# Weight sums stored in pieces of 512 bytes, their last twelve pieces in a slot of their own, and one query-weight tile in layer 1

## The chip, the core and the metric

The kernel runs on one core of one Trainium2 chip. The metric is the device time of one execution in microseconds (us), lower is better. Three runs of the kernel before took 2207.41, 2213.9 and 2215.41 us; the median is 2213.9.

Engine names in the profile: PE is the matrix engine (PEld its weight loads), DVE the vector engine, ACT the scalar engine, POOL the general engine that here only clears small regions and issues transfers, SP the queue that only issues transfers. Each engine, and each issuing queue, works through its instructions in the order in which they were written.

## The reference

Two layers, each of attention and then a feed-forward network, on 2048 tokens of width 576. The same weights serve both layers.

```
x = x + attention(layernorm(x))      # 32 heads of 18; each token looks at 8 earlier ones, 2 apart
x = x + silu(layernorm(x) @ w1) @ w2 # 576 -> 4608 -> 576
(the same two lines again)
```

Everything is in float32; the kernel gets there with pairs of fp16 halves (a high and a low part of every operand).

## The kernel before

**Stages.** The 2048 tokens are cut into four chunks of 512, so there are eight stages: stages 0 to 3 are the chunks of layer 0, stages 4 to 7 those of layer 1. A stage is attention, projection (`project`, L859 on PE, L866 on DVE), layer norm, transposition, and the feed-forward network (`ffn`). The attention of stage s+1 is meant to run on DVE while PE does the feed-forward products of stage s, and its projection lies on PE between the products of stage s.

**Two ways to the first product.** In stages 0 to 2 a tile of 128 hidden units is one run of 14 matmuls of 512 columns (L1118). From stage 3 on (`SF = 3`) two such tiles are done together by seven products in place of eight (`pair_z`, L1045: seven matmuls of 256 columns each). That needs sums and differences of the four quarters of the weights of a pair: seven combinations, each in a high and a low fp16 part. They are made once and kept in device memory, in `wts[p]` for the pairs p = 0 to 17, and loaded again by `load_wt` in every stage from 3 on (SP, L1020). The second product is L1131, and DVE adds its result to the residual at L866.

**Making the weight sums.** `prepare(p, k, t, prio, after)` does one third of a pair (k = 0, 1: 128 rows; k = 2: the last 32 rows, four times). There are 54 such pieces. Each takes a buffer ("slot") and runs

- a load of raw weights, issued by POOL (L984, L987),
- four additions on DVE (L993 to L996), the scaled high part on ACT (L998), the low part on DVE (L1003); the last one is kept in the list `preps`,
- a store into `wts[p]`, issued by POOL (L1009 for the high part, L1011 for the low part, which k = 2 has not).

The slots that a piece can have: `pw`, three of them, in the arenas `ra` and `rb`; `pk`, the two key and value tiles `kv`; `po`, the tiles `o` and `pr` of attention. Pieces 0 to 23 (`EARLY = 24`) use `pw` alone, later ones go round `pw`, `pk` and `po`. The names in the trace are those of the memory: `ra`, `rb`, `kv`, `o`, `pr`.

**Layer 1's attention.** `load_wq` (L635) loads the query, key and value weights of one of four units (8 heads each) into a `wq` tile; there are two, one in `ra` and one at the end of `rb`. The second lies in memory that every second transposed activation tile (`xt`) also uses. The load and the clearing of the `kv` tile's edge (L741, L742) are made to wait for `preps[-4:]`, the last four of the 54 pieces, because `kv`, `o` and `pr` are theirs until then. L690 is the matmul of the unit, L756 and L758 move its result to `kv` and `qt`, L768 copies the rows of neighbours, and L787 to L828 is the attention on DVE.

**What sets the order.** A planner (`Plan`) takes all operations with a guessed duration, a priority and, for transfers, a number of bytes (`nbytes`), plays them through, and writes the instructions in the order that results: each free engine takes the ready operation of the best priority whose buffers are free. So a changed cost or a changed slot moves instructions on every engine from the first piece of weight sums on.

```
def prepare(p, k, t, prio, after):
...
        op("POOL", 1.2 if k < 2 else 2.4, load, [], [(r, 0)], prio, nbytes=P * 4 * P * 6, after=after)
...
            nc.gpsimd.dma_start(d[:, :, k, :], cut_(0))
```

`wts[p]` is laid out so that the seven combinations are outermost and the five thirds (three high, two low) inside, each 128 numbers: a store writes 256 bytes at a time.

Of the kernel before, what the change touches and what calls it, by code (L numbers as in the profile page):

```python
# [16 lines left out]
P = 128  # L17
# [19 lines left out]
HT = TB // 2  # L37
HD = D // 2
SF = 3
PREP = 1.2  # L40
STEP = 1
LATE = 0.2
EARLY = 24
LNS = 512.0
HSH = 2.0 ** -5

# [229 lines left out]
def sliding_attention_silu_ffn(ctx: ExitStack, tc: tile.TileContext, x, wqkv, wo, w1, w2, out):  # L276
    nc = tc.nc
# [5 lines left out]
    op = S.op  # L283
# [8 lines left out]
    def T(b):  # L292
        return S.tags[b.tag][b.slot]
# [10 lines left out]
    def cut(a):  # L304
        return lambda v: v.rearrange("p (a b) -> p a b", a=a)
# [3 lines left out]
    QW, XW = 30 * UC, 9 * TB  # L309
    shared("ra", QW, [])  # L310
    shared("rb", 3 * XW + QW, [
        ("wq", [("ra", 0, QW), (3 * XW, 3 * XW + QW)], cut(10), True),
        ("xa", [(XW * i, XW * (i + 1)) for i in range(3)], cut(9), True),
        ("xl", [(0, XW), (35 * HT, 35 * HT + XW)], cut(9), True),
        ("x0", [(XW, 2 * XW)], cut(9), True),
# [315 lines left out]
        op("POOL", 2.8 if w.kind == "h" else 0.6, store, w.keys, [("wqs", u)], -0.6, nbytes=P * 20 * QR, after=marks[m:m + 1])  # L631

    def load_wq(u, prio):
        w = Unit("wq")
        op("SP", 0.4, lambda: nc.sync.dma_start(fl(T(w.bufs[0])), wqs[u]), [("wqs", u)], w.keys, prio, nbytes=P * 20 * QR,  # L635
           after=turned[-2:] + preps[-4:])
        return w

    WQ = (-9, -8, -7, -6)
# [81 lines left out]
    def attention(s, xT, wq, more=None):  # L721
# [4 lines left out]
        for u in range(NU):  # L726
            kv, qt = Buf("kv"), Buf("qt")
            own = [(kv, j) for j in range(NJ)]
            if wq is None:
                def fetch(kv=kv, qt=qt, u=u):  # L730
                    row = blk * TB
                    nc.scalar.dma_start(T(kv).rearrange("p a b c -> p (a b c)"),
                                        rows(kd[par][u], row, [[NJ * 2 * UC, P], [1, NI * 2 * UC]]))
                    nc.scalar.dma_start(fl(T(qt)), rows(qd[par][u], row, [[NJ * UC, P], [1, NJ * UC]]))
                op("ACT", 1.4, fetch, [("qd", c, u), ("qd0", u) if blk == 0 else ("eds", lay, par, u)],
                   own + [(qt, j) for j in range(NJ)] + [(kv, "halo"), (kv, "edge")], pr_, nbytes=P * 4 * UC * 26)
            else:
                w = wq(u)
                if blk == 0:
                    def clear(kv=kv):  # L740
                        nc.gpsimd.memset(T(kv)[0:2, 0:3], 0.0)  # L741
                        nc.gpsimd.memset(T(kv)[0:1, 3:7], 0.0)  # L742
                    op("POOL", 1.6, clear, [], [(kv, "edge")], pr_, after=turned[-2:] + preps[-4:])
                else:
                    def edge(kv=kv, u=u):
                        a, b = T(kv)[0:2, 0:3], T(kv)[0:1, 3:7]
                        e = eds[lay, par, u]
                        nc.sync.dma_start(a.rearrange("p a b c -> p (a b c)"), e[:, 2 * UC:])
                        nc.sync.dma_start(b.rearrange("p a b c -> p (a b c)"), e[1:2, :])
                    op("SP", 0.8, edge, [("eds", lay, par, u)], [(kv, "edge")], pr_, nbytes=20000, after=turned[-2:])  # L750
                for j in range(NJ):
                    m = Buf("misc")

                    def evac(j=j, m=m, u=u, kv=kv, qt=qt):
                        d = du[:, u:u + 1]
                        nc.scalar.activation(T(kv)[:, j + W - 1].rearrange("p a b -> p (a b)"), T(m)[:, UC:3 * UC],  # L756
                                             AF.Copy, scale=d)
                        nc.scalar.activation(T(qt)[:, j, :], T(m)[:, 0:UC], AF.Copy, scale=d)  # L758
                    op("PE", 2.7 if s else 2.9, lambda j=j, m=m, w=w: qkv_matmul(xT, w, j, m),
                       [(xT, j)] + w.keys, [m, (kv, j, "hold")], pr_)  # L760
                    op("ACT", 0.9, evac, [m, ("su", u)], [(kv, j), (qt, j)], pr_ - (0 if s else 9))

                def halo(kv=kv):
                    t = T(kv)

                    for p0, n, i, m in ((0, 112, 3, 4), (112, 15, 3, 4), (0, 112, 0, 3), (112, 14, 0, 3)):
                        d = 1 if i else 2
                        nc.scalar.dma_start(t[p0 + d:p0 + d + n, i:i + m], t[p0:p0 + n, 11 - m:11])  # L768
                op("ACT", 3.2, halo, own, [(kv, "halo")], pr_ - 0.2, nbytes=P * 14 * UC * 4)
                if blk == 0:  # L770
                    def save(kv=kv, u=u):
                        t = T(kv)[P - 2:P, 7:11]
                        if lay == 0:
                            nc.gpsimd.dma_start(rows(kd[par][u], W - 1 + TB - 8, [[NJ * 2 * UC, 2], [1, NJ * 2 * UC]]),
                                                t.rearrange("p a b c -> p (a b c)"))
                        else:
                            nc.gpsimd.dma_start(eds[lay, par, u], t.rearrange("p a b c -> p (a b c)"))
                    op("POOL", 0.6, save, own, [("eds", lay, par, u)], pr_, nbytes=20000)
                if more:
                    more(u, w)  # L780
# [185 lines left out]
    def prepare(p, k, t, prio, after):  # L966
# [9 lines left out]
        def cut_(i):  # L976
            return T(r)[:, (16 + 7 * i) * P:(23 + 7 * i) * P].rearrange("p (a c) -> p a c", a=7)

        def load():
            v = raw()  # L980
            for h, a in ((0, slice(0, 8, 7)), (1, slice(1, 6, 4))):
# [3 lines left out]
                else:  # L985
                    for i in range(2):
                        nc.gpsimd.dma_start(v[:, a.start + i * a.step, :], bass.AP(  # L987
                            tensor=w1.tensor, offset=at + i * P, ap=[[0, 4], [F, n], [1, P]]))
        op("POOL", 1.2 if k < 2 else 2.4, load, [], [(r, 0)], prio, nbytes=P * 4 * P * 6, after=after)

        def sums():
            v = raw()
# [12 lines left out]
        preps.append(op("DVE", 1.1, lo, [(r, 0), (r, 1), (r, 2), "st1"], [(r, 3)], prio))  # L1005

        def store():
            d = wts[p].rearrange("p (a b c) -> p a b c", a=7, b=5)
            nc.gpsimd.dma_start(d[:, :, k, :], cut_(0))  # L1009
            if k < 2:  # L1010
                nc.gpsimd.dma_start(d[:, :, 3 + k, :], cut_(1))  # L1011
        op("POOL", 1.2, store, [(r, 2), (r, 3)], [("wts", p, k)], prio, nbytes=P * 14 * P * 4)

    def load_wt(p, prio):
        ws = [Buf("w1") for _ in range(4)]
# [15 lines left out]
    def pair_z(p, xT, w, hb, key, pp, pd):  # L1031
# [8 lines left out]
        def product(z, c, m, first):  # L1040
            def mm():
                pl = [(k, k) for k in range(3)] + [(k + 3, k) for k in range(2)] + [(k, k + 3) for k in range(2)]
                for n, (i, j) in enumerate(pl):
                    q = 96 if i == j == 2 else P
                    nc.tensor.matmul(T(z)[:, 0:HT], T(w[m // 2])[0:q, m % 2 * 5 + j, :], T(xT)[0:q, 5 * c + i, :],  # L1045
                                     start=first and n == 0, stop=n == len(pl) - 1, skip_group_check=True)
            op("PE", 0.78, mm, [(xT, 0), (xT, 1), w[m // 2]], [z], pp)

# [143 lines left out]
    for s in range(NL * NC):  # L1192
        if s == SF:
            for i in range(3 * NP):
                t = ("pw", "pk", "po")[(i + i // 3) % 3 if i >= EARLY else 0]
                prepare(i // 3, i % 3, t, PREP, scaled + {"pw": [], "pk": read[-1:], "po": turned[-2:]}[t])
        ffn(s, XT[s], X[s])
        if s + 1 < NL * NC:
            front(s + 1)
# [29 lines left out]
```

## Time and profile before

| | |
|---|---|
| runs (us) | 2207.41, 2213.9, 2215.41; median 2213.9 |
| the profiled execution | 2212.85 us |
| its span, first to last instruction | 2211.0 us |
| PE busy | 2128.8 us, 96% of the span |
| DVE busy | 1647.7 us, 75% |
| ACT, POOL busy | 934.2 us, 384.1 us |
| mean granted clock of PE | 0.989 |
| moved | 419.63 MB in 294912 packets, 149176 of them under 512 B |

The profile shows one execution. Its rows give the start and the length of an instruction, the line of the kernel, what it writes and reads, how many were merged (x56), and in square brackets how long the engine sat idle before and what ended that. A row of windows gives, for a stretch of time, the busy time of each engine with its number of instructions, the granted clock of PE (1.00 is full speed), the share of the transfer engines' time and the GB/s. A row of a group ends in `| busy us, mean ns | idle before`. A row of transfers has the number, the size of one and the median time from issue to landing.

### The profile page before, as it was taken

The page shows a single profiled execution, that of the slowest core. Times are in us where ns is not written, and L with a number is a line of the kernel's source. Part 1 is how long each engine was busy: PE and PEld are TensorE (multiplying, and loading weights), DVE is VectorE, ACT ScalarE, POOL GpSimd, SP SyncE. Part 2 cuts the span into 40 slices and gives each one's busy share as a digit, 9 for nine tenths or more (in the row PEclk, how much of TensorE's full clock was granted, in tenths as well). Part 3 has the DMA queues.
Part 4 walks back from the last instruction along what each step waited for, and adds up shares of the span by engine and source line. Part 5 has one row for each costly group of instructions (what it writes and reads, how often), then busy time and mean ns, then how long its engine had stood idle before and what let it go on. Part 6 is the DMA issues. An engine that isn't in the chain of part 4 may idle for free.

```text
span 2211.0 us, 39442 instructions
## 1 busy us (share of the span) xinstructions
PE 2128.8 (96%) x15676; PEld 1532.1 (69%) x15676; DVE 1647.7 (75%) x2658; ACT 934.2 (42%) x1649; POOL 384.1 (17%) x563
## 2 busy tenths in 40 slices
PE   6889989999999999999998899999999999999998
PEld 3446555666656666687787677887778877888887
DVE  7889999899999875565896488855988569863332
ACT  7245677644243433443341443424443335333332
POOL 2124444321344452430000000000000000000000
PEclk9899999999999999999999999999999999999999
DMA  7678566795887888696355855678555865566542
GB/s 193 152 196 269 189 239 208 194 306 196 181 244 224 199 209 203 176 295 196 117 182 132 237 163 158 169 202 229 151 160 147 242 184 171 151 163 201 156 139 70
DMA packets 294912, 419.63 MB, mean 190 GB/s; under 512 B 149176, under 2 KB 180772, under 8 KB 290760
## 3 DMA queue, kind: packets, MB, share of 16 engines
q1 hardware_dynamic: 249344, 274.91, 44.6%
q0 software_dynamic: 35648, 98.79, 14.8%
q10 hardware_dynamic: 9736, 43.42, 6.2%
q8 instruction: 122, 2.00, 0.4%
q14 instruction: 62, 0.51, 0.1%
HBM read 298.47 MB, written 67.68 MB: 166 GB/s over the span
## 4 chain that ended last, share of the span: by engine, by line
PE 42%; issue 41%; DVE 7%; DMA 6%; ACT 2%; POOL 1%; SPq 1%; ACTq 0%; POOLq 0%; DVEq 0%
PE acc L1131 16%; PE z L1118 11%; PE z L690 6%; PE z L1045 6%; PE acc L859 2%; DMA oT<-yh 2%; DMA w<-in_B_w_dram 1%; DVE pr L820 1%; DMA rb<-yh 1%; DVE pr L827 1%; DVE pr L787 1%; DVE lg L791 1%; DMA qd<-hs 1%; DVE x L866 0%; DVE st L463 0%
## 5 line engine op out<-in xcount | busy, mean ns | idle before, releaser
L1131 PE MATMUL acc<-w,h 128*128 128x288 f16 x6912 | 884.7, 286 | 2.5 <-DVE x L866 2.4
L1131 PEld LDWEIGHTS <-h 128*128 128x128 f16 x6912 | 675.9, 98 | 175.7 <-issue 3.4
L1045 PE MATMUL z<-rb,w 128*128 128x256 f16 (+1 forms) x4410 | 523.7, 273 | 17.4 <-DMA rb<-o 10.0
L1045 PEld LDWEIGHTS <-w 128*128 128x128 f16 (+1 forms) x4410 | 429.8, 97 | 85.5 <-issue 16.9
L1118 PE MATMUL z<-rb,w 128*128 128x512 f16 x1512 | 336.0, 381 | 11.7 <-ACT hs L1120 5.1
L690 PEld LDWEIGHTS <-rb 128*128 128x128 f16 x1792 | 177.4, 99 | 169.7 <-issue 18.4
L1118 PEld LDWEIGHTS <-w 128*128 128x128 f16 x1512 | 148.5, 99 | 186.4 <-issue 5.0
L1025 ACT ACTIVATE h<-hs,sh 128x512 f16<-128x512 f32 x288 | 200.8, 717 | 179.2 <-PE acc L1131 174.1
L866 DVE SCALAR_TENSOR_TENSOR x<-acc,d,x 128x576 f32<-128x576 f32 x192 | 155.8, 813 | 157.3 <-PE acc L1131 156.9
L1027 DVE SCALAR_TENSOR_TENSOR h<-hs,sh,h 128x512 f16<-128x512 f32 x288 | 207.7, 746 | 70.9 <-ACT h L1025 69.8
L1050 ACT ACTIVATE hs<-z 128x256 f32<-128x256 f32 x270 | 98.7, 379 | 336.1 <-PE z L1045 304.2
L1053 DVE TENSOR_TENSOR hs<-z,hs 128x256 f32<-128x256 f32 x270 | 109.7, 418 | 148.9 <-PE z L1045 85.7
L690 PE MATMUL z<-ra,rb 128*128 128x432 f16 x952 | 186.8, 353 | 13.1 <-DMA rb<-yh 11.0
L787 DVE TENSOR_TENSOR pr<-qt,kv 128x2304 f32<-128x2304 f32 x64 | 163.3, 2552 | 42.2 <-DMA kv<-kv 33.7
L820 DVE TENSOR_TENSOR pr<-kv,pe 128x1152 f32<-128x1152 f32 x128 | 169.5, 1351 | 0.8
L791 DVE TENSOR_REDUCE lg<-pr 128x128 f32<-128x2304 f32 x64 | 162.9, 2546 | 0.5
L1120 ACT ACTIVATE hs<-z,d 128x512 f32<-128x512 f32 x108 | 73.9, 685 | 187.2 <-PE z L1118 174.2
L1145 POOL DMA_DIRECT2D out_dram<-x x16 | 8.7, 543 | 829.0 <-DVE x L866 828.6
L1057 ACT ACTIVATE hs<-hs,dt 128x256 f32<-128x256 f32 (+1 forms) x180 | 109.9, 612 | 94.1 <-DVE hs L1053 94.0
L827 DVE TENSOR_TENSOR pr<-pr 128x1152 f32<-128x1152 f32 (+1 forms) x128 | 135.1, 1056 | 3.4
L859 PE MATMUL acc<-wo,oT 128*128 128x288 f16 x896 | 115.4, 289 | 6.7 <-DMA oT<-yh 4.3
L859 PEld LDWEIGHTS <-oT 128*128 128x128 f16 x896 | 88.2, 99 | 31.5 <-DMA oT<-yh 5.1
(194 smaller groups left out, 1730.8 us busy)
## 6 DMA issues: line engine op xcount, KB each, us to landing
w<-wts SPq DMA_DIRECT2D x270, 320.0 KB
w<-w2s SPq DMA_DIRECT2D x252, 288.0 KB
w<-w1s SPq DMA_DIRECT2D x72, 320.0 KB
kv<-kd ACTq DMA_DIRECT2D x12, 1584.0 KB
w<-wts SPq DMA_DIRECT2D x90, 160.0 KB
ra<-wqs SPq DMA_DIRECT2D x13, 1080.0 KB
w1s<-w POOLq DMA_DIRECT2D x36, 320.0 KB, 3.3
w<-in_B_w_dram POOLq DMA_DIRECT2D x36, 288.0 KB, 4.6
```

The costliest lines, as they stand in the source:

```text
L690: nc.tensor.matmul(T(m)[:, :3 * UC], a, b, start=n == 0, stop=n == len(pl) - 1)
L787: nc.vector.tensor_tensor(T(pr), T(qt)[:, j:j + 2, None, :].to_broadcast([P, 2, W, UC]), win(T(kv), j, 2), op=ALU.mult)
L791: nc.vector.tensor_reduce(T(lg)[:, j:j + 2].rearrange("p a w h -> p (a w h)"), T(pr).rearrange("p a w (h d) -> p (a w h) d", d=DH), axis=A ...
L820: nc.vector.tensor_tensor(T(pr)[:, a].rearrange("p w (h d) -> p w h d", d=DH), v, T(pe)[:, j + a, :, :, None].to_broadcast([P, W, UH, DH]) ...
L827: nc.vector.tensor_tensor(t[:, :, 0:h, :], t[:, :, 0:h, :], t[:, :, h:2 * h, :], op=ALU.add)
L859: nc.tensor.matmul(T(acc)[:, h, 0:288], a, b[:, h * 288:(h + 1) * 288], start=n == 0, stop=n == len(pl) - 1)
L866: nc.vector.scalar_tensor_tensor(t, T(acc)[:, :, 0:288], d, t, op0=ALU.mult, op1=ALU.add)
L1025: op("ACT", 0.72, lambda: nc.scalar.activation(T(h)[:, 0, :], T(hs), AF.Copy, scale=sh[:, f:f + 1]), [(hs, 0), (hs, 1), key], [(h, 0)], pd)
L1027: op("DVE", 0.75, lambda: nc.vector.scalar_tensor_tensor(T(h)[:, 1, :], T(hs), sh[:, f:f + 1], T(h)[:, 0, :], op0=ALU.mult, op1=ALU.subtract),
L1045: nc.tensor.matmul(T(z)[:, 0:HT], T(w[m // 2])[0:q, m % 2 * 5 + j, :], T(xT)[0:q, 5 * c + i, :], start=first and n == 0, stop=n == len(pl) ...
L1118: nc.tensor.matmul(T(z), v, u, start=m == 0, stop=m == len(pl) - 1)
L1131: nc.tensor.matmul(T(acc)[:, h, 0:288], T(hb[q])[:, a, j * P:(j + 1) * P], T(wbs[q][0])[:, w, h * 288:(h + 1) * 288], start=q == 0 and m = ...
```

## The change

It makes four edits.

1. **Layout and store.** In `wts[p]` the first six combinations lie in three pairs, and a pair's two 128-number rows of one third lie side by side; the seventh combination of all thirds comes at the end. A store writes 512 bytes at a time for the six, and 256 for the seventh. It takes one transfer for each half's pairs and one more for the seventh: three for k = 0 and 1 (two before), two for k = 2 (one before). `product` picks its weights by the new places.
2. **Planner's costs.** The load of a piece counts 4 in place of 6 units of bytes; the store 3 (k < 2) or 1.5 (k = 2) in place of 4, and 1.8 us in place of 1.2 on POOL for k < 2.
3. **A slot of their own.** Pieces 42 to 53 (`TARDY = 42`) use only `pz`, the `rb` slot where the second `wq` tile was. No piece from 42 on uses `kv`, `o` or `pr`.
4. **Layer 1.** `load_wq` takes `wr`, the tile in `ra`, for every unit. It and the clearing of `kv` wait for pieces 36 to 41 in place of the last four.

```
+TARDY = 42
...
         ("wq", [("ra", 0, QW), (3 * XW, 3 * XW + QW)], cut(10), True),
+        ("wr", [("ra", 0, QW)], cut(10), True),
+        ("pz", [(3 * XW, 3 * XW + 30 * P)], lambda v: v, True),
...
     def load_wq(u, prio):
-        w = Unit("wq")
+        w = Unit("wr" if prio > 0 else "wq")
         op("SP", 0.4, lambda: nc.sync.dma_start(fl(T(w.bufs[0])), wqs[u]), [("wqs", u)], w.keys, prio, nbytes=P * 20 * QR,
-           after=turned[-2:] + preps[-4:])
+           after=turned[-2:] + preps[TARDY - 6:TARDY])
...
-                    op("POOL", 1.6, clear, [], [(kv, "edge")], pr_, after=turned[-2:] + preps[-4:])
+                    op("POOL", 1.6, clear, [], [(kv, "edge")], pr_, after=turned[-2:] + preps[TARDY - 6:TARDY])
...
-        op("POOL", 1.2 if k < 2 else 2.4, load, [], [(r, 0)], prio, nbytes=P * 4 * P * 6, after=after)
+        op("POOL", 1.2 if k < 2 else 2.4, load, [], [(r, 0)], prio, nbytes=P * 4 * P * 4, after=after)
...
         def store():
-            d = wts[p].rearrange("p (a b c) -> p a b c", a=7, b=5)
-            nc.gpsimd.dma_start(d[:, :, k, :], cut_(0))
-            if k < 2:
-                nc.gpsimd.dma_start(d[:, :, 3 + k, :], cut_(1))
-        op("POOL", 1.2, store, [(r, 2), (r, 3)], [("wts", p, k)], prio, nbytes=P * 14 * P * 4)
+            d = wts[p][:, 0:30 * P].rearrange("p (a b c) -> p a b c", a=3, b=5)
+            e = wts[p][:, 30 * P:].rearrange("p (b c) -> p b c", b=5)
+            for i in range(2 if k < 2 else 1):
+                nc.gpsimd.dma_start(d[:, :, 3 * i + k, :], cut_(i)[:, 0:6].rearrange("p (a b) c -> p a (b c)", a=3))
+            n = 2 if k < 2 else 1
+            c = T(r)[:, 16 * P:(16 + 7 * n) * P].rearrange("p (i a c) -> p i a c", i=n, a=7)
+            nc.gpsimd.dma_start(e[:, k::3][:, 0:n], c[:, :, 6, :])
+        op("POOL", 1.8 if k < 2 else 1.2, store, [(r, 2), (r, 3)], [("wts", p, k)], prio, nbytes=P * 14 * P * (3 if k < 2 else 1.5))
...
-                    nc.tensor.matmul(T(z)[:, 0:HT], T(w[m // 2])[0:q, m % 2 * 5 + j, :], T(xT)[0:q, 5 * c + i, :],
+                    nc.tensor.matmul(T(z)[:, 0:HT], T(w[m // 2])[0:q, 2 * j + m % 2 if m < 6 else j, :], T(xT)[0:q, 5 * c + i, :],
...
-                t = ("pw", "pk", "po")[(i + i // 3) % 3 if i >= EARLY else 0]
-                prepare(i // 3, i % 3, t, PREP, scaled + {"pw": [], "pk": read[-1:], "po": turned[-2:]}[t])
+                t = "pz" if i >= TARDY else ("pw", "pk", "po")[(i + i // 3) % 3 if i >= EARLY else 0]
+                prepare(i // 3, i % 3, t, PREP, scaled + {"pw": [], "pz": [], "pk": read[-1:], "po": turned[-2:]}[t])
```

Where the planner puts things now is seen from the order of the built program. Three places follow: SP where layer 1 begins, PE around the first projection of layer 1, and DVE where stage 2's products begin.

On SP, at the start of stage 3's products (`wts_225` holds the first pair's weight sums, `wts_230` the sixth's, `wqs_243` the first unit's query weights, `yh` the normed activations of stage 4 on their way to be transposed). Before:

```order
L1020 DMA w_94<-wts_230 128x1280
L635 DMA ra<-wqs_243 128x4320
L1020 DMA w_93<-wts_230 128x640
L635 DMA rb<-wqs_244 128x4320
L1020 DMA w_99<-wts_231 128x1280
L439 DMA_TRANSPOSE rb<-yh_88 128x9x128
```

and now:

```order
L1026 DMA w_98<-wts_225 128x1280
L638 DMA ra<-wqs_243 128x4320
L1026 DMA w_96<-wts_225 128x1280
L879 DMA w_104<-w2s_223 128x1152
L879 DMA w_105<-w2s_224 128x1152
```

The first load of query weights has moved from among the sixth pair's loads to among the first pair's; the second unit's load no longer stands beside it but behind the four transposes, among the loads of `wts_231`.

On DVE, at the start of the feed-forward network of stage 2, the rows up to its first addition to the residual, `x_66` (`rb`, `ra` are weight sums in their slots, `h` the hidden units, `pr`, `lg`, `mx`, `pe` the attention of stage 3). Before:

```order
L1027 SCALAR_TENSOR_TENSOR h_115<-hs_120,sh,h_115 128x512
L800 TENSOR_REDUCE mx_85<-lg_82 128x32
L801 TENSOR_TENSOR lg_82<-lg_82,mx_85 128x256
L1027 SCALAR_TENSOR_TENSOR h_112<-hs_121,sh,h_112 128x512
L805 TENSOR_REDUCE mx_86<-pe_84 128x32
L806 RECIPROCAL mx_86<-mx_86 128x32
L807 TENSOR_TENSOR pe_84<-pe_84,mx_86 128x256
L820 TENSOR_TENSOR pr_79<-kv_77,pe_84 128x1152 x2
L866 SCALAR_TENSOR_TENSOR x_66<-acc_133,d_297,x_66 128x576
```

and now:

```order
L1033 SCALAR_TENSOR_TENSOR h_112<-hs_121,sh,h_112 128x512
L1006 SCALAR_TENSOR_TENSOR rb<-rb,st_294 128x896
L1006 SCALAR_TENSOR_TENSOR ra<-ra,st_294 128x896
L996 TENSOR_TENSOR rb<-rb 128x128
L997 TENSOR_TENSOR rb<-rb 128x128
L998 TENSOR_TENSOR rb<-rb 128x128
L999 TENSOR_TENSOR rb<-rb 128x128
L1033 SCALAR_TENSOR_TENSOR h_116<-hs_122,sh,h_116 128x512
L869 SCALAR_TENSOR_TENSOR x_66<-acc_133,d_297,x_66 128x576
```

Two finished pieces of weight sums and the additions of a third stand where the softmax and the last products of the attention stood. Over the whole program up to this addition 29 low parts (L1003, now L1006) and 30 sets of additions stand ahead of it, where it was 23 and 23.

On PE, the first product of stage 4 (`pair_z`) comes behind the last projection of stage 4. Between the two stood 156 matmuls of L1131 and nothing else; now 276 of L1131 and 70 of L1045 stand there. The projection itself has moved forward.

## The prediction

> **What bounds the kernel now.** I read the page first: how busy is each engine?
>
> ```profile
> span 2211.0 us, 39442 instructions
> PE 2128.8 (96%) x15676; PEld 1532.1 (69%) x15676; DVE 1647.7 (75%) x2658; ACT 934.2 (42%) x1649; POOL 384.1 (17%) x563
> ```
>
> PE is the bound; it idles 82.2 us in all, so only the removal of its waits can shorten the run, and each new wait lengthens it. Next I read the windows, to see where those 82 us lie. The two programs have the same order on DVE up to about 570 us of this trace and on PE up to about 597, so what is lost there stays. Behind it two places stand out (PE, PEld, DVE, ACT, POOL busy; PE's clock; DMA share; GB/s):
>
> ```profile
> 600.00:725.00 125.00, 125.00 (x799) 78.03 (x797) 120.90 (x170) 53.61 (x66) 54.02 (x69) 1.00 0.81 239
> 775.00:800.00 25.00, 21.00 (x147) 14.79 (x146) 14.59 (x29) 3.38 (x4) 15.39 (x20) 0.93 0.99 207
> 1190.63:1240.63 50.00, 37.05 (x299) 29.47 (x297) 30.80 (x83) 13.11 (x22) 5.86 (x8) 0.93 0.78 221
> 1471.00:1521.00 50.00, 49.23 (x409) 39.35 (x407) 27.28 (x69) 18.44 (x39) 2.21 (x4) 1.00 0.96 295
> ```
>
> The third row is the start of layer 1, stage 4: PE idles 12.95 us of 50, and its clock drops to 0.93. The fourth is the same place in stage 5, where it idles 0.77. From 600 to 725 us PE never waits, but DVE is busy 120.90 of 125 us: there the second engine is as full as the first.
>
> The timeline of PE shows what it waits for in stage 4, and the rate of L1045 when nothing holds it:
>
> ```profile
> 1031.48 5.62 PE L1045 MATMUL z<-rb,w 128*128 128x256 f16 x49
> ...
> 1190.63 19.27 PE L1131 MATMUL acc<-w,h 128*128 128x288 f16 x156
> 1218.58 3.35 PE L1045 MATMUL z<-rb,w 128*128 128x256 f16 x16 [8.68 <-DMA rb<-o]
> ```
>
> The last projection ends at 1190.6; then there are 156 matmuls (19.27 us) to do while the layer norm and its transposes (`rb<-o`) run, which take until 1218.6. Chain: 28 us; cover: 19 us. The chain is late because layer 1's attention began late. The timelines of DVE, POOL and SP:
>
> ```profile
> 976.28 1.15 DVE L1003 SCALAR_TENSOR_TENSOR o<-o,st 128x896 f16<-128x896 f32 x1
> 978.67 0.81 POOL L741 MEMSET kv<- 2x864 f32 x1
> 978.95 0.44 SPq L635 DMA_DIRECT2D ra<-wqs  x1
> 1024.09 2.56 DVE L787 TENSOR_TENSOR pr<-qt,kv 128x2304 f32<-128x2304 f32 x1 [17.05 <-DMA kv<-kv]
> ```
>
> The clearing of `kv` and the load of the query weights start 2 us behind the last weight sum, and DVE sits idle for 17 us until the first keys are there.
>
> **The change part by part.** *The earlier attention (edits 3 and 4).* By the order of the built program 276 matmuls of L1131 and 70 of L1045 now stand between the last projection of stage 4 and its first product: 276 x 19.27/156 + 70 x 5.62/49 = 34.1 + 8.0 = 42 us of cover against a chain of 28. What is lost there now: in those 50 us PE did 299 matmuls, 156 of which took 19.27 us and 143 of which would take 143 x 0.115 = 16.4, so 50 - 35.7 = 14.3 us (12.95 of idling, the rest at the lower clock). What stays is the 0.8 us of stage 5. Gain 13.5 us, bounds 12 and 15; next late is nothing at that place, as 14 us of cover are to spare.
>
> *Weight sums ahead of other work on DVE (edits 1 to 3).* The smaller byte counts and the new slot let the planner pull the sums forward, into the stretch in which DVE is full. In order of time, the rows that price them (DVE's group is of 600 to 1250 us), with PE beside the first addition of stage 2 (739.00):
>
> ```profile
> L1003 DVE SCALAR_TENSOR_TENSOR rb<-rb,st 128x896 f16<-128x896 f32 x10 | 11.4, 1144 | 0.0
> 727.86 2.54 DVE L791 TENSOR_REDUCE lg<-pr 128x128 f32<-128x2304 f32 x1
> 736.46 2.63 DVE L820 TENSOR_TENSOR pr<-kv,pe 128x1152 f32<-128x1152 f32 x2
> 739.00 0.81 DVE L866 SCALAR_TENSOR_TENSOR x<-acc,d,x 128x576 f32<-128x576 f32 x1
> 742.28 0.28 DVE L993 TENSOR_TENSOR rb<-rb 128x128 f32<-128x128 f32 x1
> 743.22 0.28 DVE L993 TENSOR_TENSOR rb<-rb 128x128 f32<-128x128 f32 x1
> 731.55 13.39 PE L1131 MATMUL acc<-w,h 128*128 128x288 f16 x108
> L1118 PE MATMUL z<-rb,w 128*128 128x512 f16 x1512 | 336.0, 381 | 11.7 <-ACT hs L1120 5.1
> ```
>
> One set of four additions takes 743.22 - 742.28 = 0.94 us, a low part 1.14. By the order, seven more sets and six more low parts stand ahead of that addition: 7 x 0.94 + 6 x 1.14 = 13.4 us. Behind it have gone one reduction (2.54), two products (2.63) and a softmax of five small rows, for which I estimate 2 us: 7.2. DVE comes 6.2 us later. PE's third group of 36 needs this addition, since two sums take turns in `acc`; it began at 731.55 + 72 x 13.39/108 = 740.5, and the addition ended at 739.81, so there are 0.7 us of room. PE has 14 more matmuls of L1118 ahead of it now (14 x 336.0/1512 = 3.1 us), and DVE has up to 4.1 idle us between 600 and 725 to absorb the rest. So 6.2 - 0.7 - 3.1 = 2.4 if none of the idle time helps, 0 if it does; the store's landing may also come later than the planner thinks and stop DVE at a set, so I take +3, bounds 0 and 6.
>
> *The projection of stage 3.* It follows 50 us later, with both of its waits in view (DVE's last half, SP's transposes in stage 2 and the same ones in stage 3, then PE's two halves):
>
> ```profile
> 757.09 0.51 DVE L846 TENSOR_SCALAR yh<-o,so 128x576 f16<-128x576 f32 x1
> 758.88 11.74 SPq L439 DMA_TRANSPOSE oT<-yh  x2
> 1166.86 3.06 SPq L439 DMA_TRANSPOSE oT<-yh  x2
> 780.68 7.02 PE L859 MATMUL acc<-wo,oT 128*128 128x288 f16 x56 [1.35 <-DVE x L866]
> 794.76 7.48 PE L859 MATMUL acc<-wo,oT 128*128 128x288 f16 x46 [2.65 <-DMA oT<-yh]
> ```
>
> It loses 1.35 + 2.65 = 4.0 us today. By the order five more low parts, six more sets and three additions of `h` stand ahead of its half at 757.09 (5 x 1.14 + 6 x 0.94 = 11.3; an `h` is 512 columns where a low part is 896, so an estimated 0.65 each: 13.3 us), and PE is there about 3 us sooner. Against that, two transposes that took 11.74 us here took 3.06 where fewer small stores were under way, which would give back up to 8.7. That would be 13.3 + 3 - 8.7 = 7.6 us late, if nothing were to spare; but the half was normed 23 us ahead of PE and its transposes were issued after 13.5 of them, so up to 10 us of room lie ahead of the first wait, none ahead of the second. I take +2, bounds -4 (the waits go) and +8.
>
> *The first unit of layer 1.* It stands 98 matmuls of L1045 and 66 of L1131 earlier in PE's order, 98 x 0.115 + 66 x 0.124 = 19 us, and its query weights come five pairs' loads earlier on SP. Its first matmuls before, and a stretch in which units already follow one another through one tile (columns as in the windows above):
>
> ```profile
> 996.56 2.72 PE L690 MATMUL z<-ra,rb 128*128 128x432 f16 x14
> 1250.00:1480.00 230.00, 229.83 (x1847) 180.14 (x1845) 170.15 (x236) 87.90 (x165) 7.18 (x11) 1.00 0.59 163
> ra<-wqs SPq DMA_DIRECT2D x13, 1080.0 KB
> rb<-wqs SPq DMA_DIRECT2D x4, 1080.0 KB
> ```
>
> At 996.56 it did not wait. Its activations are normed behind the additions of stage 2's products, the last of which (943.57, below) ended 52 us ahead of it; 19 us sooner leaves 33 for the norm and the transposes, where the chain at stage 4's start took 28. That is enough on paper, but the norm stands on DVE among the sums that are now spread over this stretch: I take +2, bounds 0 and 8. The one tile costs nothing in stages 5 and 6, where 230 us pass with 0.17 us of PE idle: of 17 loads only 4 ever went to `rb`. In stage 4 the second unit has 49 matmuls of L1045 and 12 of L1131 behind the first (7 us) in which to load; I take 0, bounds 0 and 3. The Trainium skill, "Trainium Kernel Development and Optimization", section Best Practices, has operands double-buffered so that transfers run beside compute; by it this edit would be a loss, and the row of 230 us speaks against that for 12 of layer 1's 16 units.
>
> *Stores and issues (edit 1).* The page's transfers before:
>
> ```profile
> DMA packets 294912, 419.63 MB, mean 190 GB/s; under 512 B 149176, under 2 KB 180772, under 8 KB 290760
> wts<-rb POOLq DMA_DIRECT2D x35, 224.0 KB, 4.7
> rb<-in_B_w_dram POOLq DMA_DIRECT2D x24, 128.0 KB, 5.0
> wts<-pr POOLq DMA_DIRECT2D x9, 224.0 KB, 5.5
> kv<-in_B_w_dram POOLq DMA_DIRECT2D x16, 64.0 KB, 7.4
> 772.57 0.94 POOL L1009 DMA_DIRECT2D wts<-kv  x1 [1.00 <-DVE kv L1003]
> ```
>
> 54 more issues x 0.94 = 51 us on POOL, which is busy 384 of 2211 and which only the next piece's load waits for: 0. Half of all packets are under 512 bytes; the stores of the sums are 18 pairs x 35 rows x 128 partitions = 80640 of them, and six sevenths of these become half as many of 512. The Trainium skill, "DMA: Bandwidth & Descriptors", section Specifications, asks for 512 bytes or more, below which a write must read first. By it the stores get cheaper and the transposes beside them too; no run here shows how much, so it enters no term: it speaks for the first rival.
>
> *Sum.* -13.5 + 3 + 2 + 2 = -6.5. The profiled execution took 2212.85 us, so 2206.35; the median is 1.05 above it, so 2207.4.
>
> **The rivals.** *A: the whole gain.* With the transposes at their 3.06 us and DVE's idle time taken up, the two middle terms vanish or turn: -13.5 and up to -4, 2196.4 to 2200.4, say 2198. For it: in the 230 us of stage 5 no transpose stops PE, and the earlier sums themselves cost PE only where DVE is full. Against it: 120.90 of 125 us busy on DVE.
>
> *B: the one slot is too slow, and the run gets slower.* Twelve pieces go through `pz` one after the other, eleven turnarounds, each of which needs the store to land before the next load. With the rows for a store's issue, a load's issue and the high part, and the two additions between which the pieces lie:
>
> ```profile
> 867.03 1.62 POOL L984 DMA_DIRECT2D pr<-in_B_w_dram  x2
> 975.21 1.04 ACT L998 ACTIVATE o<-o,st 128x896 f16<-128x896 f32 x1
> 748.50 1.53 DVE L866 SCALAR_TENSOR_TENSOR x<-acc,d,x 128x576 f32<-128x576 f32 x2
> 943.57 0.82 DVE L866 SCALAR_TENSOR_TENSOR x<-acc,d,x 128x576 f32<-128x576 f32 x1 [3.59 <-PE acc L1131]
> ```
>
> A turn takes 3 x 0.94 + 4.7 (landing) + 1.62 + 5.0 (landing) + 0.94 + 1.04 + 1.14 = 17.3 us; the stretch has 943.57 - 748.50 = 195 us, 17.7 for each of eleven. With the landings of the other slots, 5.5 and 7.4, a turn takes 20.5, and DVE, which works in order, stands at each set 2.8 us longer, in all 31 us; PE waits with it at the next addition, and less than the 7 us that PE has ahead at the end is absorbed: -6.5 + 24 = 17.5 over, 2231. It decides from about 19 us a turn. For it: the two numbers lie 0.4 us apart. Against it: the planner has other work between, and stores of 512 bytes should not land later than those of 256.
>
> *C: the one tile stops PE.* Four loads lose their second tile; a load of 1080 KB takes 5 us at the 221 GB/s of stage 4's window, against the 7 us between the first units, exposed where the queue is behind: at most 2 each for the four, 8 in all, 2215.
>
> *D: the start of stage 4 does not go.* If a store or load holds the attention where it was, only what it costs elsewhere shows: -13.5 falls away, 2213.9 + 7 = 2221.
>
> **How the numbers follow.** The forecast has 0.45, A 0.33, B 0.12, C and D 0.05 each. What a measurement of this kernel can tell from no change is about 0.5%, 11 us: 2202.8 and 2225. Faster by more: A and a small part of the forecast's own spread (0.04): 0.37. Slower by more: B and a part of D, 0.14. The rest, 0.49, is the same. The bounds of the terms in the forecast alone give 2195 to 2221. The range is 2194 to 2224: it takes in A, C and D, and leaves out B and the ends.
>
> **What would show it.** Right: between the last projection of stage 4 and its first L1045, PE idles under 2 us with L1131 and L1045 rows between (13.5 gained). DVE has no idle time of more than 3 us in stage 2 that ends in a DMA of `rb` (B is wrong), and PE shows waits of 2 to 5 us that end in `x` L866 between 730 and 760 (the DVE term) and in `oT` near 785 (the projection). The first L690 of layer 1 follows with a wait of 0 to 8 us on `rb<-yh`. A shows as PE without any of these; B as DVE rows L993 with some 2.8 us before each, ended by a DMA; C as L690 rows that wait for `ra<-wqs`. The forecast is wrong in kind if PE idles more than 100 us in all, or if its idle time before 600 us changes by more than 5 us, for then something acts that the order does not show.

## The result, and the profile after

| | before | changed |
|---|---|---|
| runs (us), six each | 2207.41 to 2218.11 | 2195.82 to 2203.91 |
| median | 2214.65 | 2199.32 |
| ratio, 95% interval | | 0.9937 [0.9917, 0.9958] |
| profiled execution: span | 2211.0 | 2202.1 |

The changed kernel is 14 us faster by the ratio. Its profiled execution is the slowest of its six runs (2203.91). Ratios here and below leave out two slow runs, one of e9_two_tiles (12470.19 us) and one of the kernel before beside it (2265.99). First the page's busy times:

```profile
span 2202.1 us, 39553 instructions
PE 2127.9 (97%) x15676; PEld 1532.1 (70%) x15676; DVE 1649.3 (75%) x2658; ACT 932.9 (42%) x1649; POOL 403.4 (18%) x617
```

PE's busy time is the same within 1 us; its idle time went from 82.2 to 74.2, and these 8.0 us are most of the 8.9 between the spans. The windows that answer to those of before (columns as there), and one more:

```profile
600.00:725.00 125.00, 125.00 (x797) 77.71 (x795) 121.95 (x182) 53.64 (x67) 74.15 (x105) 1.00 0.81 249
775.00:800.00 25.00, 21.16 (x164) 16.20 (x163) 18.12 (x38) 4.73 (x5) 14.24 (x21) 0.96 0.69 115
1190.00:1250.00 60.00, 59.35 (x486) 47.10 (x485) 28.57 (x72) 20.18 (x44) 5.76 (x8) 1.00 0.83 250
1285.00:1295.00 10.00, 4.54 (x25) 3.06 (x22) 3.85 (x6) 1.38 (x3) 0.00 (x0) 0.72 0.82 230
```

The start of stage 4 idles 0.65 us in 60, where it was 12.95 in 50. Stage 3's projection, near 775 to 800, idles 3.84, where it was 4.0. And there is a hole that was not there: 5.46 us near 1290, in stage 5. PE's timeline at stage 3's projection, at stage 4's start and at the hole:

```profile
777.99 7.02 PE L862 MATMUL acc<-wo,oT 128*128 128x288 f16 x56
790.58 3.60 PE L862 MATMUL acc<-wo,oT 128*128 128x288 f16 x28 [1.16 <-DVE rb L996]
796.86 5.26 PE L862 MATMUL acc<-wo,oT 128*128 128x288 f16 x28 [2.67 <-DVE x L869]
...
1162.90 3.59 PE L862 MATMUL acc<-wo,oT 128*128 128x288 f16 x28
1166.33 5.54 PE L1051 MATMUL z<-rb,w 128*128 128x256 f16 x49
...
1208.15 5.54 PE L1051 MATMUL z<-rb,w 128*128 128x256 f16 x49
...
1280.33 5.31 PE L1137 MATMUL acc<-w,h 128*128 128x288 f16 x42
1291.10 3.15 PE L1051 MATMUL z<-rb,w 128*128 128x256 f16 x14 [5.46 <-ACT hs L1056]
```

The last projection of stage 4 ends at 1166.3 and stage 4's first product starts at 1208.15 without a wait: 42 us of other products lie between. Layer 1's attention is earlier, as DVE's, POOL's and SP's timelines have it:

```profile
946.09 1.14 DVE L1006 SCALAR_TENSOR_TENSOR rb<-rb,st 32x896 f16<-32x896 f32 x1
905.00 0.81 POOL L744 MEMSET kv<- 2x864 f32 x1
896.66 0.37 SPq L638 DMA_DIRECT2D ra<-wqs  x1
1001.80 2.56 DVE L790 TENSOR_TENSOR pr<-qt,kv 128x2304 f32<-128x2304 f32 x1 [1.53 <-DMA kv<-kv]
```

The last weight sum starts at 946 (before: 976), the first unit's load goes out at 897 (979), and attention starts at 1002 (1024). So far this is what the prediction's first term said. What it does not show is which of the four edits did it.

### The profile page after: what moved, and what is told of

It is laid out like the page before. It is cut to its first block, busy times and chain, and to the rows that moved or that the text cites. A ratio compares the mean times of both kernels' runs of the same rounds, so it can differ in the third digit from the quotient of the medians.

```text
span 2202.1 us, 39553 instructions
## 1 busy us (share of the span) xinstructions
PE 2127.9 (97%) x15676; PEld 1532.1 (70%) x15676; DVE 1649.3 (75%) x2658; ACT 932.9 (42%) x1649; POOL 403.4 (18%) x617
## 2 busy tenths in 40 slices
DMA packets 295201, 419.64 MB, mean 191 GB/s; under 512 B 150040, under 2 KB 181636, under 8 KB 291048
## 3 DMA queue, kind: packets, MB, share of 16 engines
q0 software_dynamic: 35936, 98.79, 14.1%
## 4 chain that ended last, share of the span: by engine, by line
PE 73%; issue 11%; DVE 8%; DMA 6%; ACT 1%; POOL 1%; ACTq 0%; SPq 0%; DVEq 0%; POOLq 0%
PE acc L1137 30%; PE z L1051 17%; PE z L1124 12%; PE z L693 10%; PE acc L862 4%; DMA w<-in_B_w_dram 1%; DVE pr L823 1%; DMA rb<-yh 1%; DVE pr L830 1%; DVE pr L790 1%; DVE lg L794 1%; DVE x L869 1%; DMA qd<-hs 1%; DMA w<-w2s 1%; DVE w L933 1%
## 5 line engine op out<-in xcount | busy, mean ns | idle before, releaser
L1124 PE MATMUL z<-rb,w 128*128 128x512 f16 x1512 | 335.7, 382 | 12.1 <-ACT hs L1126 5.3
L1124 PEld LDWEIGHTS <-w 128*128 128x128 f16 x1512 | 148.5, 99 | 187.5 <-issue 5.4
L693 PE MATMUL z<-ra,rb 128*128 128x432 f16 x1176 | 231.0, 353 | 16.8 <-DMA rb<-yh 14.7
```

Of the source, the lines that this page charges most:

```text
L693: nc.tensor.matmul(T(m)[:, :3 * UC], a, b, start=n == 0, stop=n == len(pl) - 1)
L1124: nc.tensor.matmul(T(z), v, u, start=m == 0, stop=m == len(pl) - 1)
```

## The experiments

Ten kernels, in three groups that each ran on one chip and share the runs of the kernel before. Ratios are to the kernel before, with 95% intervals.

| run | what it is | ratio | PE idle 1190 to 1250 us (stage 4's start) | longest wait of PE 1250 to 1400 us (stage 5) |
|---|---|---|---|---|
| e1_again | changed kernel | 0.9951 [0.9936, 0.9967] | 0.6 | 5.55 |
| e2_small_packets | changed order, old stores | 0.9926 [0.9908, 0.9945] | 0.7 | 5.33 |
| e3_big_packets | before, new stores | 0.9989 [0.9976, 1.0003] | 12.5 | under 0.5 |
| e4_no_slot | edits 1 and 2 | 0.9916 [0.9904, 0.9929] | 2.3 | 0.54 |
| e5_costs_only | edit 2 | 0.9909 [0.9893, 0.9925] | 2.2 | 0.55 |
| e6_slot_only | edits 3 and 4 | 1.0032 [1.0020, 1.0043] | 20.6 | 2.16 |
| e7_fourth_copy | changed, one copy moved | 0.9895 [0.9882, 0.9909] | 0.7 | under 0.5 |
| e8_load_number | one number of edit 2 | 0.9987 [0.9972, 1.0002] | 11.2 | 1.68 |
| e9_two_tiles | changed, two tiles | 0.9965 [0.9953, 0.9977] | 1.2 | 5.25 |
| e10_last_four | changed, old wait | 0.9967 [0.9953, 0.9981] | 0.8 | 1.22 |

**The changed kernel again (e1_again).** No edit. Expected:

> The changed kernel once more, unedited. If the 5.46 us for which PE waits on ACT near 1291 us, and the 3.4 us that the profiled execution lost before 400 us, belong to the program, both are in this profile too and the profiled execution takes about 2204 us. If they belong to that one execution, PE's idle time behind 600 us is under 10 us and the profiled execution takes 2195 to 2200. Either way the ratio to before is 0.992 to 0.996.

The hole came again, 5.55 us at 1293, and in e2_small_packets, which has the same order, 5.33: it belongs to the program. The loss before 400 us does not: PE idled 50.5 us there in the profile of before, and 51.9 to 56.6 in the eleven others, whose order on PE is the same up to there.

**The same order with the old stores (e2_small_packets).**

```diff
-            d = wts[p][:, 0:30 * P].rearrange("p (a b c) -> p a b c", a=3, b=5)
...
+            d = wts[p].rearrange("p (a b c) -> p a b c", a=7, b=5)
+            nc.gpsimd.dma_start(d[:, :, k, :], cut_(0))
+            if k < 2:
+                nc.gpsimd.dma_start(d[:, :, 3 + k, :], cut_(1))
...
-                    nc.tensor.matmul(T(z)[:, 0:HT], T(w[m // 2])[0:q, 2 * j + m % 2 if m < 6 else j, :], T(xT)[0:q, 5 * c + i, :],
+                    nc.tensor.matmul(T(z)[:, 0:HT], T(w[m // 2])[0:q, m % 2 * 5 + j, :], T(xT)[0:q, 5 * c + i, :],
```

> The changed kernel with the layout and the stores of before (256 bytes at a time), and the planner's numbers of the changed kernel: PE, DVE, ACT and SP have the changed kernel's order row by row, only the stores differ. Theory 1 (the gain is the earlier attention of layer 1, which the order gives): the ratio is that of the changed kernel, 0.992 to 0.996, and PE idles under 2 us at stage 4's start. Rival (the 512-byte stores themselves bring it, as sums and transposes land sooner): 0.998 or more, with DVE rows L996 that wait for DMA in stage 2 and the one slot's turnaround over 19 us.

With 256-byte pieces and 54 issues fewer it is not slower than the changed kernel in the same group (0.9926 and 0.9951, intervals that overlap). The rival falls.

**The old order with the new stores (e3_big_packets).** The reverse edit on the kernel before: layout and store of edit 1, the planner's numbers as they were.

> The kernel before with the new layout and the new stores alone; the planner's numbers are those of before, so the order of all engines is before's, POOL's extra issues apart. Theory 1: 0.999 to 1.001; the 13 us of idle PE at stage 4's start stay. Rival (the stores themselves bring it): 0.996 or less, and the two transposes that took 11.74 us near 759 us take under 6.

0.9989, an interval that holds 1. The gain is not in the stores themselves. Rows of transfers (count, size, median us from issue to landing) and the row of POOL's queue q0 (packets, MB, share of the transfer engines' time), of the changed kernel and then of e2_small_packets:

```profile
wts<-rb POOLq DMA_DIRECT2D x50, 192.0 KB, 3.7
wts<-rb POOLq DMA_DIRECT2D x18, 64.0 KB, 3.8
q0 software_dynamic: 35936, 98.79, 14.1%
```

```profile
wts<-rb POOLq DMA_DIRECT2D x50, 224.0 KB, 4.4
q0 software_dynamic: 35648, 98.79, 14.7%
```

The landing times give no rate, since 64 KB took 3.8 us where 192 KB took 3.7. In share of time the queue took 14.1% with the new stores and 14.7% with the old; in the order of before it took 14.6% (e3_big_packets) and 14.8%. The larger pieces save a little transfer time, and no time of the kernel that shows.

**Without edits 3 and 4 (e4_no_slot).**

```diff
-                t = "pz" if i >= TARDY else ("pw", "pk", "po")[(i + i // 3) % 3 if i >= EARLY else 0]
+                t = ("pw", "pk", "po")[(i + i // 3) % 3 if i >= EARLY else 0]
...
-        w = Unit("wr" if prio > 0 else "wq")
+        w = Unit("wq")
...
-           after=turned[-2:] + preps[TARDY - 6:TARDY])
+           after=turned[-2:] + preps[-4:])
```

(The last line is changed in both places.)

> The changed kernel without edits 3 and 4: no slot of its own, layer 1's loads wait for the last four pieces, two query-weight tiles; layout, stores and the planner's byte counts are the changed kernel's. My prediction put the earlier attention down to edits 3 and 4: then stage 4's start still loses over 8 us and the ratio is 0.998 to 1.000. Rival (the byte counts of edit 2 alone move it; in this build 270 matmuls of L1131 and 63 of L1045 stand behind the last projection of stage 4): PE idles under 2 us there and the ratio is 0.992 to 0.996.

0.9916, which is below the changed kernel's 0.9951 in the same group, with intervals that don't overlap. PE idles 2.3 us at stage 4's start, just over the 2 expected. My attribution falls: the attention comes early without a slot of its own and with the old wait.

**Edit 2 alone (e5_costs_only).** The kernel before with three numbers:

```diff
-        op("POOL", 1.2 if k < 2 else 2.4, load, [], [(r, 0)], prio, nbytes=P * 4 * P * 6, after=after)
+        op("POOL", 1.2 if k < 2 else 2.4, load, [], [(r, 0)], prio, nbytes=P * 4 * P * 4, after=after)
...
-        op("POOL", 1.2, store, [(r, 2), (r, 3)], [("wts", p, k)], prio, nbytes=P * 14 * P * 4)
+        op("POOL", 1.8 if k < 2 else 1.2, store, [(r, 2), (r, 3)], [("wts", p, k)], prio, nbytes=P * 14 * P * (3 if k < 2 else 1.5))
```

> The kernel before with edit 2 alone: the three numbers of the planner (bytes of a load 6 to 4, bytes of a store 4 to 3 and 1.5, POOL's time of a store 1.2 to 1.8); layout, stores, slots, waits and tiles are those of before. Theory 2 (the numbers alone make the gain, by the order): 0.990 to 0.994, like the kernel without edits 3 and 4, with PE idle under 2 us at stage 4's start. My prediction's attribution (the gain comes by edits 3 and 4): 0.998 to 1.000.

0.9909: the whole gain, and more than the changed kernel has of it. DVE, SP and PE of this run:

```profile
920.71 1.15 DVE L1003 SCALAR_TENSOR_TENSOR o<-o,st 128x896 f16<-128x896 f32 x1
920.76 0.43 SPq L635 DMA_DIRECT2D ra<-wqs  x1
1159.48 3.59 PE L859 MATMUL acc<-wo,oT 128*128 128x288 f16 x28
1203.23 5.54 PE L1045 MATMUL z<-rb,w 128*128 128x256 f16 x49
```

The last sum starts at 921, where it was 976, with stores, slots and waits as before. The planner had counted 384 KB for a piece's load, which is two transfers of 128.0 KB in the rows, and 896 KB for its store, which is two of 224.0. With 256 and 672 KB counted it places the pieces earlier, and with them all that waits for the last four.

**Edits 3 and 4 alone (e6_slot_only).** The changed kernel with edit 1 undone as in e2_small_packets and edit 2 undone as in the diff above, read from + to -.

> Edits 3 and 4 alone: slot of its own, the earlier wait and the one tile, with the layout, the stores and the planner's numbers of before. My prediction's attribution: about 0.994. Theory 2: by the order only 24 matmuls of L1131 are left behind the last projection of stage 4, 24 x 0.1235 = 3 us of cover against a chain of 28, so PE idles some 25 us there in place of 13 and the ratio is 1.003 to 1.007.

1.0032, slower, by the low edge of what was expected; PE idles 20.6 us at stage 4's start. PE at stage 4's start, and DVE's last sum:

```profile
1204.13 3.10 PE L1137 MATMUL acc<-w,h 128*128 128x288 f16 x24
1226.74 3.60 PE L1051 MATMUL z<-rb,w 128*128 128x256 f16 x16 [19.51 <-DMA rb<-o]
```

```profile
1039.10 1.14 DVE L1006 SCALAR_TENSOR_TENSOR rb<-rb,st 32x896 f16<-32x896 f32 x1
```

With the old numbers the planner spreads the twelve pieces of the one slot until 1039, and 24 matmuls are all the cover (work that PE has while the chain runs) that is left: 3.1 us against a chain that took 22.6 here.

**One number (e8_load_number).** The first of the two lines of edit 2 alone.

> The kernel before with one number changed, the bytes of a load 6 to 4. By the order 192 matmuls of L1131 stand behind the last projection of stage 4: 192 x 0.1235 = 23.7 us of cover against a chain of 28. If cover against chain sets the loss, PE idles 3 to 6 us there (13 before) and the ratio is 0.995 to 0.997. If the loss goes altogether whenever the sums end earlier, 0.992 to 0.994.

0.9987, above both ranges, with an interval that holds 1. The first wait is what cover against chain gives:

```profile
1179.00 23.68 PE L1131 MATMUL acc<-w,h 128*128 128x288 f16 x192
1209.32 3.39 PE L1045 MATMUL z<-rb,w 128*128 128x256 f16 x16 [6.63 <-DMA rb<-o]
```

The chain took 30.3 us, the cover 23.7: 6.6. Behind it PE lost 4.6 us more in small waits while its next inputs came, which my 3 to 6 left out; 11.2 us were lost in place of 13. Its median gained 3.7 us; the profile had 2.3 us less idle time than before behind 400 us. The last sum starts at 958 here (before: 976), so earlier sums do not remove the loss by themselves: the cover has to exceed the chain.

**The fourth copy (e7_fourth_copy).** What is the hole in stage 5? ACT, of the changed kernel:

```profile
1278.21 2.09 ACT L1031 ACTIVATE h<-hs,sh 128x512 f16<-128x512 f32 x3
1279.68 10.94 ACTq L771 DMA_DIRECT2D kv<-kv  x4
1290.66 0.38 ACT L1056 ACTIVATE hs<-z 128x256 f32<-128x256 f32 x1 [10.37 <-DMA w<-w2s]
```

L771 are four copies that fill the neighbours' rows of `kv`; ACT issues them, which takes 2.9 to 3.9 us in most units and took 10.94 here. (The bracket puts ACT's wait down to a transfer of `w2s`, but the row above shows what ACT was at: the copies.) The built program shows what each copy waits for. A transfer raises a completion mark, a counter, when it has landed. In this program the transfers of SP and ACT take their marks from one set of eight (DMAHW0 to DMAHW7), and a transfer first waits until the mark's last user has landed:

```
957 L771 DMA kv_77<-kv_77 112x1152 [waits DMAHW7_49,DMAHW4_49,Activation_49]
958 L771 DMA kv_77<-kv_77 15x1152 [waits DMAHW2_49]
959 L771 DMA kv_77<-kv_77 112x864 [waits DMAHW5_49]
960 L771 DMA kv_77<-kv_77 14x864 [waits DMAHW7_49]
```

The first copy took mark 7, and the fourth takes 7 again: it waits for the first to land. In the trace the first copy goes out at 1279.68, raises its mark for the last time at 1289.79, and the fourth goes out at 1289.81. SP issues a load of query weights and six more loads around the first:

```profile
1277.55 0.32 SPq L638 DMA_DIRECT2D ra<-wqs  x1
1278.28 5.92 SPq L879 DMA_DIRECT2D w<-w2s  x6
```

The query weights and two of the six go out ahead of the first copy: 1080 + 2 x 288 = 1656 KB, about 7 us at the 230 GB/s of that window (an estimate). The other four go out while it is under way. The experiment moves this one copy, of this one unit, to POOL's queue, where it doesn't wait for the first:

```diff
-                        nc.scalar.dma_start(t[p0 + d:p0 + d + n, i:i + m], t[p0:p0 + n, 11 - m:11])
+                        q = nc.gpsimd if s == 5 and u == 1 and n == 14 else nc.scalar
+                        q.dma_start(t[p0 + d:p0 + d + n, i:i + m], t[p0:p0 + n, 11 - m:11])
```

> The changed kernel with one of its transfers issued by POOL in place of ACT: the fourth of the four copies that fill the neighbours' rows of kv, for the second unit of stage 5 alone. Theory (ACT stands behind the fourth copy, which by the built program waits for the completion mark of the first, and the first lands late behind the load of query weights; PE waits for ACT): PE's wait of 5.5 us near 1290 is under 1.5 us, the ratio to the changed kernel 0.997 to 0.998. Rival (the transfers' backlog itself holds ACT or PE): the wait stays over 4 us and the time is the changed kernel's.

ACT and PE at that place:

```profile
1276.77 2.02 ACTq L772 DMA_DIRECT2D kv<-kv  x3
1278.83 0.38 ACT L1057 ACTIVATE hs<-z 128x256 f32<-128x256 f32 x1 [1.44 <-DVE h L1034]
```

```profile
1277.41 5.31 PE L1138 MATMUL acc<-w,h 128*128 128x288 f16 x42
1282.56 1.70 PE L1052 MATMUL z<-rb,w 128*128 128x256 f16 x14
```

The hole is gone, though the first copy lands as late as before: it goes out at 1276.77 and raises its mark until 1286.67, 9.9 us later. So it was the wait for the mark, and not the backlog of transfers.

At 0.9895 the kernel is as fast as edit 2 alone in the same group (2192.09 and 2194.22 us). Against the changed kernel's 0.9951 in another group that is 12 us, more than the 0.997 to 0.998 expected, and more than the wait of 5.5. PE has the same order in both programs, so their profiles can be compared row by row: the work that takes 75.2 us in the changed kernel (1246.4 to 1321.5) takes 67.1 us here (1243.5 to 1310.5). The hole costs 8.1 us, the wait and a lower clock behind it: from 1285 to 1300 the mean granted clock is 0.77 there and 1.00 here. Of the 13.1 us between the two spans (2202.1 and 2189.1), 2.9 arise ahead of this stretch and 2.1 behind it; their cause stays open.

**Two tiles, and the old wait (e9_two_tiles, e10_last_four).** The one tile could still be behind the hole, since the load of query weights that delays the copies goes out when the tile comes free. Two builds cross the two causes. In the first, `load_wq` takes `Unit("wq")`, so there are two tiles, and the fourth copy still shares its mark with the first. In the second both waits read `preps[-4:]`: one tile, and no copy shares a mark with its own unit's first.

> The changed kernel with two query-weight tiles (the slot of its own and the earlier wait are kept). In this build the fourth copy for the neighbours' rows in the second unit of stage 5 again waits for the mark of the first, with the load of query weights and six loads of L879 ahead of it on SP. Theory (that wait is what the changed kernel loses in stage 5, not the one tile): PE waits 4 to 7 us near 1290, ratio 0.993 to 0.996. Rival (the one tile is the cause): no wait over 1.5 us there, ratio 0.989 to 0.993.

> The changed kernel with the wait of before: layer 1's loads and the clearing wait for the last four pieces, which now come from the one slot; one tile. In this build no copy waits for the first of its own unit. Theory: no wait of PE over 1.5 us in stage 5, and at stage 4's start 282 matmuls of L1137 and 28 of L1051 (38 us) cover a chain of 23 to 30, so 0.989 to 0.993, no worse than the changed kernel. Rival (the earlier wait of edit 4 is what makes the gain): PE idles over 6 us at stage 4's start, 0.996 or more.

PE in the one, then in the other:

```profile
1282.80 2.37 PE L1137 MATMUL acc<-w,h 128*128 128x288 f16 x18
1290.41 1.65 PE L1051 MATMUL z<-rb,w 128*128 128x256 f16 x7 [5.25 <-ACT hs L1056]
```

```profile
1449.08 26.62 PE L1137 MATMUL acc<-w,h 128*128 128x288 f16 x216
1479.11 1.24 PE L1051 MATMUL z<-rb,w 128*128 128x256 f16 x6 [3.41 <-DMA rb<-o]
```

Two tiles and a shared mark: 5.25 us, with a ratio of 0.9965, just over the 0.993 to 0.996 expected. One tile and no shared mark: no wait over 1.22 between 1250 and 1400, and 0.8 us idle at stage 4's start, so the earlier wait of edit 4 is not needed there either. But its ratio of 0.9967 misses what I expected: this order leaves only 216 matmuls behind the last projection of stage 5, 26.6 us against a chain of 30.0, at the place where the changed kernel has 288 + 70. PE waits 3.4 us there and idles 8.1 us in all from 1450 to 1530, where the changed kernel idles 0.65.

## Why the prediction came out as it did

The time fell within the range, 8 us below the forecast of 2207.4 and within 2 of rival A's 2198. It is one of the gains of over 11 us, to which the prediction gave 0.37. That it lies within the range is in part luck: a loss that no term had, the wait for the mark in stage 5, stands in the place of the 7 us of three terms that did not come. Without that wait (e7_fourth_copy, in another group) the median is 2192.09, below the range's 2194.

**Earlier attention, -13.5.** Right in size and in the way it works, cover against chain: 12.3 us of idle time less in the 60 us around stage 4's start, and the clock there back from 0.94 to 1.00. Wrong in its cause, "edits 3 and 4": e4_no_slot and e5_costs_only have the gain without them, and e6_slot_only has the loss with them alone. The order of the changed program showed the cover, but I read a sum of edits from it; each edit's own order, which can be built without a chip, has 24, 270 and 276 matmuls of cover for edits 3 and 4, for edit 2, and for all, and would have shown it.

**Weight sums ahead on DVE, +3.** Measured 0: PE never idles from 600 to 740 us in either profile. At 597 us, up to which the two programs have the same order on PE, this execution was already 1.8 us behind. Without these 1.8, DVE came 2.4 us later at the first addition of stage 2 (743.24 for 739.00), where 6.2 were predicted. Its idle time from 600 to 740 went from 7.0 to 3.2 us, and that is the difference. PE's third group of 36 came 3.0 us later (745.3 for 740.5), since 14 matmuls of L1124 now stand between the first group and the second; 3.1 were predicted. In DVE's and PE's rows:

```profile
743.24 0.82 DVE L869 SCALAR_TENSOR_TENSOR x<-acc,d,x 128x576 f32<-128x576 f32 x1
```

```profile
740.83 13.39 PE L1137 MATMUL acc<-w,h 128*128 128x288 f16 x108
```

The addition ended at 744.06 and the group began at 740.83 + 36 x 0.124 = 745.3, so 1.2 us of room are left. The parts of the term were right. The step that failed is the choice between its ends: 0 if DVE's idle time helps, 2.4 if it doesn't. It helped in full, and I took 3.

**Projection of stage 3, +2.** Measured -0.2, but by another way. The first two transposes are nearly as short as rival A had them (3.06 us), on SP's queue:

```profile
770.33 4.63 SPq L442 DMA_TRANSPOSE oT<-yh  x2
```

4.63 us where it was 11.74, and the first half waits no more. The stores are not the reason, since the same two took 10.34 us in e3_big_packets. But the second half now waits for DVE, which stands at additions whose raw weights have not landed:

```profile
790.24 0.29 DVE L996 TENSOR_TENSOR rb<-rb 128x128 f32<-128x128 f32 x1 [3.28 <-DMA rb<-in_B_w_dram]
793.97 0.29 DVE L997 TENSOR_TENSOR kv<-kv 128x128 f32<-128x128 f32 x1 [2.07 <-DMA kv<-in_B_w_dram]
```

The first of these is the third piece of the new slot: its load was issued only at 781.77, since POOL, in order, first stood 5.15 us for a store of `kv`. That is rival B's mechanism in one turn of eleven, and its 3.28 us are over the 3 that the prediction gave as B's sign. Over all, its twelve low parts run from 754.28 to 946.09, 17.4 us a turn against the 17.3 predicted and the 19 from which it would have decided. From 725 to 800 us the changed kernel idles 3.84 us; three other profiles with its order on PE idle 3.50, 1.69 and 3.33 (e1_again, e2_small_packets, e7_fourth_copy). Without the slot it is 0.2 in e5_costs_only and 1.2 in e4_no_slot, whose order differs elsewhere too, so that the slot is the likely cause and not a shown one.

**First unit, +2.** Measured 0: it starts at 976.81 without a wait, as it did at 996.56. PE idles 0.8 us from 940 to 1030, where it idled 3.5, but the waits that went are ones for DVE and ACT between 953 and 960 and at 1030, which the prediction did not price.

**The one tile, 0.** Right: e9_two_tiles has the same hole, and e10_last_four has one tile and none. Rival C had the loads of query weights stop PE in stage 4; what PE lost is in stage 5, and by one completion mark.

**Stores, 0.** Right (e2, e3). But the count behind it was wrong: I took 80640 packets for the stores, and packets under 512 bytes went from 149176 to 150040, by 54 issues x 16, so that the page's packets are not the pieces of 256 bytes. In the trace's records no packet of POOL's queue has 256 or 512 bytes, with either layout.

Put together: behind 597 us the profiled execution gains 10.7 us on the one before, 10.4 of them idle time. Of these, 12.3 are gained at stage 4's start and 2.7 between 940 and 1030, 5.5 are lost in stage 5, and 0.9 are gained elsewhere. With the 1.8 us by which it was behind at 597, that leaves the 8.9 between the spans (2211.0 and 2202.1). The medians lie 11 to 15 us apart; the difference is within the scatter of single executions, 1 to 6 us before 400 us alone. Rival A's number was met with half its mechanism: the transposes are shorter, and the three middle terms come to near 0, but not all waits at the projection went, and the number holds the 8 us of stage 5, which A did not have.

## What to carry to other kernels

Where a planner sets the order, build each edit alone and compare orders before pricing anything: here three of the planner's numbers made the whole gain, and the slot and the earlier wait without them made a loss. At a stage's start, set the work that stands between (cover) against the chain that must finish; the loss is what is missing, and a little more, for inputs that arrive one by one (4.3 us more in the kernel before, 4.6 in e8_load_number, 1.1 in e6_slot_only). An engine that issues transfers can stand behind one of its own: look in the built program at what each issue waits for.

The fastest versions here are edit 2 alone (0.9909) and the changed kernel with one copy on POOL's queue (0.9895). Both lie below the changed kernel's 0.9937 and 0.9951, which were measured in other groups.

## What the runs showed that I had not expected

- Stores in pieces of 512 bytes bring no time that shows (0.9951 with them, 0.9926 without, in the same order); POOL's queue takes 14.1% of the transfer engines' time in place of 14.7%. The Trainium skill, "DMA: Bandwidth & Descriptors", section Specifications, has 512 bytes as the least for line rate. These runs show a small effect in that direction, and none on the kernel.
- One wait for a completion mark held ACT for 10 us and PE for 5.2 to 5.6, in four profiles of three builds, and there is none in the profile where only that copy's queue was changed. With the lower clock behind it, it cost the kernel 8.1 us.
